# Quarter loads, an earlier third q, and k^T v portions moved between exchange and values in an attention and expert kernel

## The chip, the cores and the metric

One core of a Trainium2 chip. The metric is the device time of one run in microseconds; lower is better.

## What is computed

The reference has two parts, one feeding the other. The first is a linear attention over 8 batches, 8 heads, 576 tokens and 64 features per head, all in FP32:

```python
kv = np.einsum('bhsd,bhse->bhde', k, v)
out = np.einsum('bhsd,bhde->bhse', q, kv)
rms = np.sqrt(np.mean(out * out, axis=-1, keepdims=True) + 1e-06)
x = (out / rms * g_norm)            # then laid out as 4608 tokens of 512
```

The second is a mixture of 8 experts on those 4608 tokens. A token whose product with `w_skip` is not positive keeps its value. Every other token takes the expert with the largest logit, goes through `relu(x @ w1) @ w2` (512 to 1024 to 512), and adds the result weighed by its gate.

## The kernel before, in words

**Attention** takes the first 106 us or so. A token is 4 tiles wide: head pairs are two partition halves (`a`), and four pairs lie in the free dimension as `2u + w`. A load of one batch's k, v or q fills a tile of 128 partitions x 4 x 9 x 64 numbers (1.18 MB). `load_part` (L115 to L120) issues half of it, two of the four pairs, as one DMA of 576 KB on SyncE's queue (SP); `load_kv` issues the halves of k and v alternately, `load_q` the two of q. k and v have three buffers each, q has two. DMAs share eight completion semaphores in turn, so the issue of one waits on SP until the one eight places before it has landed.

Per batch b there are these pieces of work:

- `state(b, some)`, a **portion** of k^T v (L379): of the batch's 18 chunks it takes `some`, four matmuls of 64x64 for each (the trace shows eight passes, as FP32 takes two). The first nine chunks need the first half of k and v, the other nine the second. With the last chunk, ScalarE copies the sum out of PSUM (L386).
- `state_t(b)` transposes it (L393, then ScalarE's copy to kvT, L396), `state_m(b)` multiplies with the gate weights (L402, copy L405).
- `state_s(b)`, the **exchange** (L411, 64x64 tiles, then ScalarE's copies L415), puts each head pair's matrix on the other partition half as well. The batch's values need L415.

The values are taken in 36 units. Each batch has four (two groups of tokens, two head groups u); after four batches, two tail units take the ninth token group of all four. Units 0 to 15 are batches 0 to 3, 16 and 17 the tail, then 18 to 33 and 34, 35 in the same way. A batch's first units are thus 0, 4, 8, 12, 18, 22, 26, 30.

The order of work is written out by hand: TensorE (PE) runs what the program lists, in that order. One loop step n does:

```python
turn(n + 1)          # PE: transpose q (L460); ScalarE: copy qT (L463). None for tail units
root(n - 1)          # ScalarE: square root of the mean squares (L529)
jobs(n, "early")
values(n)            # PE: L479 and L498, or L508 for a tail unit; ScalarE: squares (L514)
jobs(n, "mid")
norm(n - 1)          # VectorE: reciprocal (L536), scale (L545), which frees the PSUM bank
squares(n)           # VectorE: sum of squares (L522)
jobs(n, "pe")
... jobs(n, "end")   # here also loads and stores are issued
```

`values(n)` writes one of two PSUM buffers (`o_ps`), freed by L545 of unit n - 2. `at(step, part, job)` puts a job into a step. `portions[b]` gives for batch b the step of its first portion and the number of chunks in each portion, one portion per step, all of them in part "pe", behind the values. The step after the last portion has `state_t` ("early") and `state_m` ("pe"); the next has the exchange, "early" when it is the batch's first unit, else "pe". `load_kv(b + 3)` goes to the end of the step with b's transpose (step 0 for batch 0), `load_q(b + 2)` to the end of the batch's third unit.

Beside this run, in VectorE's and GpSimd's time: the weighing of values by g_norm (L615), stores of x on SP (L650) and GpSimd (L646), and, from step 12 on, the choice of experts (`gating`: VectorE, and a ranking on PE, L693 to L699), a few instructions in each step. At the very start `dense` matmuls (L170) on constants fill PE's time between the first pieces of work.

**The experts** take the rest: tokens are gathered by indirect DMAs, the two layers run in `layer_1`, `layer_2`, `fast_1` and `fast_2` (L1176, L1188, L1256), and the weights of the next expert are loaded (L336, L346) when PE has done with their buffer.

Of the kernel before, what the change touches and what calls it, by code (L numbers as in the profile page):

```python
# [8 lines left out]
FP32 = mybir.dt.float32  # L9
# [8 lines left out]
def kernel(  # L18
# [44 lines left out]
    B, H, S, D = q.shape  # L63
    DM = H * D
    N = B * S
    P = 128
    C = S // 64
# [30 lines left out]
    kv_pool = attn.enter_context(tc.tile_pool(name="kv", bufs=3))  # L98
# [13 lines left out]

    kts, vts, qts = {}, {}, {}

    def load_part(t, src, b, u):  # L115

        js = slice(2 * u, 2 * u + 2)
        nc.sync.dma_start(
            out=t[:, js, :, :].rearrange("p j c d -> p j (c d)"),
            in_=src[b].rearrange("(j a) (p c) d -> (a p) j (c d)", a=2, c=C)[:, js, :])  # L120

    def load(pool, tag, src, b):
        t = pool.tile([P, 4, C, D], FP32, tag=tag, name=tag)
        for u in range(2):
            load_part(t, src, b, u)
        return t

    def load_kv(b):
        if b < B:
            for name, to in (("k", kts), ("v", vts)):  # L130
                to[b] = kv_pool.tile([P, 4, C, D], FP32, tag=name, name=name)
            for u in range(2):
                for src, t in ((k, kts[b]), (v, vts[b])):
                    load_part(t, src, b, u)

    def load_q(b):
        if b < B:
            qts[b] = load(q_pool, "q", q, b)
# [4 lines left out]


    load_kv(0)
    load_q(0)

# [19 lines left out]
    def dense(count, ps=warm_ps):  # L167

        for _ in range(count):
            nc.tensor.matmul(out=ps[:, :], lhsT=ones[:, :],  # L170
                             rhs=ones[:, :].unsqueeze(1).to_broadcast([P, 4, P]), start=True, stop=True)
# [33 lines left out]
    for i in range(KVD):  # L205
        t = kvd_pool.tile([P, 2, 2, 2, PK], FP32, name=f"kvd{i}")
# [87 lines left out]
    for lo, m, _ in runs:  # L294

        if m < P and (lo, m) not in again:
            t = keep.tile([P, P], FP32, name=f"again{lo}_{m}")
# [57 lines left out]
    def own(b, w):  # L355

        return kvds[b % KVD][w * 64:(w + 1) * 64, :, w, w, :]
# [7 lines left out]
    def ends_of(x):  # L365

        ap = [list(d) for d in x.ap]
        assert ap[-1] == [1, PK]
        return bass.AP(x.tensor, x.offset, ap[:-1] + [[PK - G, 2], [1, G]])

    def state(b, some):

        kt, vt = kts[b], vts[b]
        for i in some:
            u, c = divmod(i, C)
            for w in range(2):
                for a in range(2):
                    r = slice(a * 64, (a + 1) * 64)
                    nc.tensor.matmul(  # L379
                        out=sum_ps[w * 64:(w + 1) * 64, a, u, :],  # L380
                        lhsT=kt[r, 2 * u + w, c, :], rhs=vt[r, 2 * u + w, c, :],
                        start=(c == 0), stop=(c == C - 1), skip_group_check=True)
        if some.stop < 2 * C:
            return
        for w in range(2):
            nc.scalar.copy(out=own(b, w)[:, :, G:G + 2 * D].rearrange("p u (a d) -> p a u d", a=2),  # L386
                           in_=sum_ps[w * 64:(w + 1) * 64, :, :, :])

    def state_t(b):
        for u in range(2):  # L390
            for w in range(2):
                r = slice(w * 64, (w + 1) * 64)
                nc.tensor.matmul(out=kvT_ps[:, u, r], lhsT=kvds[b % KVD][:, u, w, w, G:G + 2 * D],  # L393
                                 rhs=ident[:, r], start=True, stop=True)
        kvT = att_pool.tile([P, 2, P], FP32, tag="kvT", name="kvT", bufs=1)
        nc.scalar.copy(out=kvT[:, :, :], in_=kvT_ps)  # L396
        kvTs[b] = kvT

    def state_m(b):
        kvT = kvTs.pop(b)  # L400
        for u in range(2):
            nc.tensor.matmul(out=lg_ps[:, u, :, :, :], lhsT=kvT[:, u, :], rhs=gw_b[:, u, :, :, :],  # L402
                             start=True, stop=True)
        for w in range(2):
            nc.scalar.copy(out=ends_of(own(b, w)), in_=lg_ps[w * 64:(w + 1) * 64, :, :, w, :])  # L405

    def state_s(b):

        for w in range(2):
            r, o = slice(w * 64, (w + 1) * 64), slice((1 - w) * 64, (2 - w) * 64)  # L410
            nc.tensor.matmul(out=sw_ps[o, :], lhsT=ident[r, r], rhs=own(b, w), start=True, stop=True,  # L411
                             skip_group_check=True)
        for w in range(2):
            o = slice((1 - w) * 64, (2 - w) * 64)
            nc.scalar.copy(out=kvds[b % KVD][o, :, w, 1 - w, :],  # L415
                           in_=sw_ps[o, :].rearrange("p (u k) -> p u k", u=2))
# [25 lines left out]
    def at(step, part, job):  # L442
        todo.setdefault((step, part), []).append(job)
# [7 lines left out]
    def turn(n):  # L451
        _, b, i, u = units[n]
        if i is None:
            qTs[n] = q8s[b][:, u, :, :, :]
            return
        ps = ps_q.tile([P, 2, 2, 2, 64], FP32, tag="q", name="q_ps")
        for w in range(2):
            for hf in range(2):
                c = 4 * i + 2 * hf
                nc.tensor.transpose(out=ps[:, w, :, hf, :], in_=qts[b][:, 2 * u + w, c:c + 2, :],  # L460
                                    identity=ident[:, :])
        qT = att_pool.tile([P, 2, 2, P], FP32, tag="qT", name="qT")
        nc.scalar.copy(out=qT[:, :, :, :].rearrange("p w a t -> p (w a t)"),  # L463
                       in_=ps[:, :, :, :, :].rearrange("p w a h t -> p (w a h t)"))
        qTs[n] = qT
# [353 lines left out]
    def slot_rows(cols, pool, tag):  # L819

        n = cols.stop - cols.start
        rows = pool.tile([P, n], I32, tag=f"rows{tag}", name="rows")
        nc.vector.tensor_single_scalar(out=rows[:, :], in_=srow[:, cols], scalar=float(N),
                                       op=ALU.add)
        src = pool.tile([P, n], I32, tag=f"src{tag}", name="src")
        nc.vector.scalar_tensor_tensor(out=src[:, :], in0=rows[:, :], scalar=N, in1=rows[:, :],
                                       op0=ALU.is_lt, op1=ALU.mult)
        return rows, src
# [64 lines left out]
    def early():  # L893
# [41 lines left out]
        yield "mid", put  # L935

    load_kv(1)
    load_q(1)
    load_kv(2)


# [7 lines left out]
    starts = {}  # L949
    for n, (_, b, i, _) in enumerate(units):  # L950
        if i is not None:
# [2 lines left out]
    dense(4)  # L954
    state(0, range(C, 2 * C))
    dense(5)
    turn(0)
    state_t(0)
    state_m(0)
    turn(1)  # L960
    state_s(0)

    portions = {1: (1, (10, 8)), 2: (4, (6, 6, 6)), 3: (7, (5, 6, 7)), 4: (11, (3, 4, 4, 4, 3)),
                5: (16, (3, 2, 6, 7)), 6: (20, (4, 4, 5, 5)), 7: (24, (4, 4, 5, 5))}
    over = 0
    for b, n in starts.items():
        if b:
            step, counts = portions[b]
            i = 0
            for count in counts:  # L970
                at(step, "pe", lambda b=b, some=range(i, i + count): state(b, some))
                i += count
                step += 1
            assert i == 2 * C and step < n and step - len(counts) > over - 1
            at(step, "early", lambda b=b: state_t(b))
            at(step, "pe", lambda b=b: state_m(b))
            at(step + 1, "early" if step + 1 == n else "pe", lambda b=b: state_s(b))
            over = step
        at(over, "end", lambda b=b: load_kv(b + 3))

        at(n + 2, "end", lambda b=b: load_q(b + 2))

    def gating(g):

        yield from choose(g)
        yield lambda: rank(g)
        numbers = number(g)
        yield next(numbers)
        if g == LAST - 1:
            yield from rank_experts()  # L990
            load_weights(0, wpool_a, later=True)
        yield from numbers
        if g == LAST - 1:
            yield from early()
# [60 lines left out]
    with tc.tile_pool(name="wpool_b", bufs=1, reuse_waits="tile") as wpool_b, \  # L1055
# [491 lines left out]
        rows, src = slot_rows(slice(0, NCOL), gat_pool, "")  # L1547
# [34 lines left out]
        with tc.If(n_rounds > 1):  # L1582
            with tc.For_i(1, n_rounds, 1):
# [12 lines left out]
                rows, src = slot_rows(slice(0, NCOL), slot_pool, "")  # L1596
# [35 lines left out]
```

## Time and profile before

| | |
|---|---|
| median of 3 runs | 374.82 us (374.59 to 375.59) |
| the profiled execution | 374.1 us, of which the span is 372.2 us |
| granted TensorE clock | 0.998 |
| TensorE matmul busy | 361.7 us, 97% of the span |
| VectorE, ScalarE, GpSimd busy | 243.4, 145.9, 119.9 us |
| loads of k, v, q | 16 DMAs each, 576 KB, median 10.0, 10.8, 10.7 us to landing |

Times in the profile count from the start of the span. A row of the timeline gives start, duration, engine, line, operation, tiles written and read, shape, the number of instructions merged, and in brackets the engine's idle time before it and the work that ended it.

### The profile page before, as it was taken

Reading aid. Unit: us, or ns where it says so; the run is one execution under the profiler, and the core shown is the slowest. Engines: PE = TensorE matmul, PEld = TensorE weight load, DVE = VectorE, ACT = ScalarE, POOL = GpSimd, SP = SyncE. Lnnn points to the kernel's source line nnn. Section 1 sums busy time; section 2 is a strip of 40 time slices with the busy share of each in tenths; the row PEclk is TensorE's granted clock in tenths of the full one; section 3 lists DMA queues with packets and bytes.
Section 4 is the critical chain, followed back from the end, with each engine's and each line's share of the span. In section 5 each row is a group of like instructions: output and inputs, shape, how many; then the busy total and the mean of one; then the engine's idle time right before and its main releaser. Section 6 shows DMA issues by size and latency. Waiting matters only on the chain.

```text
span 372.2 us, 9661 instructions
## 1 busy us (share of the span) xinstructions
PE 361.7 (97%) x3859; PEld 314.4 (84%) x3859; DVE 243.4 (65%) x630; ACT 145.9 (39%) x398; POOL 119.9 (32%) x189
## 2 busy tenths in 40 slices
PE   8999999999999999999999999999999999999994
PEld 4687797898979779689879987998988998999983
DVE  3355367767788753875856685876876876878831
ACT  2466576676777132224303511431430440441420
POOL 7035467655767253223022303303202302102003
PEclk9999999999999999999999999999999999999999
DMA  8999999997489449974608264672762762601001
GB/s 289 393 391 390 402 404 395 406 393 232 135 316 311 115 119 324 397 249 168 224 32 274 64 227 139 205 242 75 253 233 48 276 232 55 257 3 42 16 1 54
DMA packets 32039, 81.70 MB, mean 219 GB/s; under 512 B 2474, under 2 KB 2482, under 8 KB 31988
## 3 DMA queue, kind: packets, MB, share of 16 engines
q1 hardware_dynamic: 28176, 69.47, 52.5%
q0 software_dynamic: 3792, 11.53, 9.2%
q8 instruction: 32, 0.52, 0.6%
q14 instruction: 19, 0.16, 0.1%
q10 hardware_dynamic: 20, 0.02, 0.0%
HBM read 66.80 MB, written 14.48 MB: 218 GB/s over the span
## 4 chain that ended last, share of the span: by engine, by line
PE 87%; issue 5%; ACT 3%; POOL 2%; DVE 1%; POOLq 0%; ACTq 0%; DVEq 0%
PE bank L1256 45%; PE bank L1188 9%; PE o_ps L498 7%; PE sum_ps L379 5%; PE q_ps L460 4%; PE bank L1176 4%; PE g_ps L393 2%; PE q_ps L170 2%; PE bank L1157 2%; PE g_ps L856 1%; PE g_ps L411 1%; ACT qT L463 1%; PE o_ps L508 1%; PE q_ps L856 1%; PE g_ps L402 1%
## 5 line engine op out<-in xcount | busy, mean ns | idle before, releaser
L1266 ACT COPY p<-bank 128x128 f32<-128x128 f32 (+6 forms) x70 | 20.8, 297 | 99.4 <-PE bank L1256 97.6
L1256 PE MATMUL bank<-xt,w 128*128 128x128 f32 (+5 forms) x336 | 55.4, 288 | 0.0
L1387 POOL DMA_INDIRECT out_dram<-xg,rows x14 | 14.0, 999 | 119.5 <-DVE xg L1384 108.4
L615 POOL TENSOR_TENSOR xb<-xl,g_b 128x512 f32<-128x512 f32 x34 | 41.3, 1216 | 32.1 <-DVE rs L536 30.3
L1256 PEld LDWEIGHTS bank<-xt,w 128*128 128x128 f32 x336 | 47.0, 190 | 1.9 <-DVE bank L1260 1.4
L1260 DVE TENSOR_TENSOR bank<-bank,p 128x128 f32<-128x128 f32 (+6 forms) x70 | 23.5, 336 | 30.3 <-PE bank L1256 29.4
L498 PE MATMUL o_ps<-kvd,qT 128*128 128x146 f32 x240 | 35.8, 290 | 1.0 <-ACT kvd L415 0.7
L1256 PE MATMUL bank<-xs,s 128*128 128x128 f32 (+5 forms) x224 | 36.7, 288 | 0.0
L522 DVE TENSOR_REDUCE rs<-sq 128x8 f32<-128x512 f32 x36 | 24.6, 682 | 14.5 <-ACT sq L514 14.4
L498 PEld LDWEIGHTS o_ps<-kvd,qT 128*128 128x128 f32 x240 | 31.5, 188 | 2.0 <-ACT kvd L415 1.5
L1256 PEld LDWEIGHTS bank<-xs,s 128*128 128x128 f32 x224 | 31.1, 190 | 1.0 <-ACT p L1266 0.8
L1188 PE MATMUL bank<-w,ht 128*32 128x128 f32 (+2 forms) x424 | 29.9, 313 | 0.0
L545 DVE TENSOR_TENSOR xl<-o_ps,rs 128x584 f32<-128x584 f32 x32 | 24.5, 767 | 4.3 <-DVE rs L536 0.5
L1188 PEld LDWEIGHTS bank<-w,ht 128*32 128x32 f32 (+2 forms) x424 | 18.2, 119 | 10.7 <-issue 7.6
L1256 PE MATMUL bank<-t,ht 128*128 128x256 f32 x112 | 27.0, 384 | 0.0
L1256 PE MATMUL bank<-w,ht 128*128 128x256 f32 x112 | 26.5, 380 | 0.0
L514 ACT ACTIVATE sq<-o_ps 128x512 f32<-128x512 f32 x34 | 20.3, 597 | 15.0 <-PE o_ps L498 14.4
L1148 POOL DMA_INDIRECT xg<-out_dram,src x14 | 15.3, 1092 | 33.0 <-DMA out_dram<-xg,rows 17.3
L1256 PE MATMUL bank<-t,hs 128*128 128x256 f32 x112 | 25.3, 379 | 0.0
L379 PE MATMUL sum_ps<-v,k 64*64 64x64 f32 x1152 | 24.7, 223 | 0.4 <-issue 0.4
L379 PEld LDWEIGHTS sum_ps<-v,k 64*64 64x64 f32 x1152 | 20.9, 134 | 4.3 <-issue 1.8
L1256 PEld LDWEIGHTS bank<-t,ht 128*128 128x128 f32 x112 | 20.8, 190 | 3.9 <-issue 1.2
(224 smaller groups left out, 677.2 us busy)
## 6 DMA issues: line engine op xcount, KB each, us to landing
w<-in_moe_w_dram SPq DMA_DIRECT2D x16, 2048.0 KB, 8.9
k<-in_k_dram SPq DMA_DIRECT2D x16, 576.0 KB, 10.0
v<-in_v_dram SPq DMA_DIRECT2D x16, 576.0 KB, 10.8
q<-in_q_dram SPq DMA_DIRECT2D x16, 576.0 KB, 10.7
out_dram<-xb SPq DMA_DIRECT2D x29, 256.0 KB, 9.4
out_dram<-xb POOLq DMA_DIRECT2D x7, 256.0 KB, 6.4
xg<-out_dram,src POOLq DMA_INDIRECT x16, 3.7
out_dram<-xg,rows POOLq DMA_INDIRECT x16, 5.9
```

The costliest lines, as they stand in the source:

```text
L379: nc.tensor.matmul(out=sum_ps[w * 64:(w + 1) * 64, a, u, :], lhsT=kt[r, 2 * u + w, c, :], rhs=vt[r, 2 * u + w, c, :], start=(c == 0), stop ...
L460: nc.tensor.transpose(out=ps[:, w, :, hf, :], in_=qts[b][:, 2 * u + w, c:c + 2, :], identity=ident[:, :])
L498: mm = nc.tensor.matmul(out=ps[:, w, 0:2 * PK].rearrange("p (r k) -> p r k", r=2)[:, :, cols], lhsT=qT[:, w, a, :], rhs=kvds[b % KVD][:, u ...
L514: nc.scalar.activation(out=sq[:, :, :, :], in_=heads(ps, G, G + 2 * D), func=ACT.Square)
L522: nc.vector.tensor_reduce(out=rs[:, :, :], in_=sq[:, :, :, :].rearrange("p x y (a d) -> p x (y a) d", a=2), axis=AX.X, op=ALU.add)
L545: nc.vector.tensor_tensor(out=xl[:, :, :, :].rearrange("p x y (a k) -> p x (y a) k", a=2), in0=ps[:, :, 0:2 * PK].rearrange("p x (h k) -> ...
L615: late.append((lambda eng: eng.tensor_tensor(out=xb[:, :, 4 * u * D:(4 * u + 4) * D].rearrange("p r (w x) -> p r w x", w=2), in0=xl[:, :, ...
L1148: nc.gpsimd.indirect_dma_start(out=x_of(xg, off, m), out_offset=None, in_=cut_rows(m)[:, :], in_offset=bass.IndirectOffsetOnAxis(ap=idx[:, ...
L1188: nc.tensor.matmul(out=yps[q * m:(q + 1) * m, 0:n], lhsT=ht(f)[:, off:off + m], rhs=w_sb[r][1][:, f, q * n:(q + 1) * n], start=(f == 0), s ...
L1256: nc.tensor.matmul(out=out, lhsT=lhsT(i), rhs=rhs(i), start=start and i == 0, stop=i == k - 1, skip_group_check=True)
L1260: nc.vector.tensor_tensor(out=to, in0=x, in1=y, op=ALU.add)
L1266: nc.scalar.copy(out=t, in_=x)
```

## The change

Loads: each of k, v and q comes in quarters of 288 KB, one pair each, instead of halves. Batch 3's k and v are issued in two parts: the first two quarters of each where all of it was, the other two behind the third q (batch 2's).

Order: at the start `state_t(0)` stands ahead of `turn(0)`. The first portions of batch 2 (step 4), batch 3 (step 8) and batch 5 (step 16) move from behind the step's values to ahead of them; in steps 4 and 8 that is behind the exchange. Batch 4 has three portions (5, 6, 7 chunks) instead of five, so that its transpose, multiplication and exchange come two steps earlier (14 and 15), and so does the issue of batch 7's k and v. Batch 5's portions hold 8, 4, 3, 3 chunks instead of 3, 2, 6, 7. The last batch's transpose goes behind the values of its step, and its multiplication into the next step, behind that step's turn.

```diff
-    def load_part(t, src, b, u):
-        js = slice(2 * u, 2 * u + 2)
+    def load_part(t, src, b, j):
+        js = slice(j, j + 1)
...
-        for u in range(2):
-            load_part(t, src, b, u)
+        for j in range(4):
+            load_part(t, src, b, j)
...
-    def load_kv(b):
+    def load_kv(b, js=range(4)):
         if b < B:
-            for name, to in (("k", kts), ("v", vts)):
-                to[b] = kv_pool.tile([P, 4, C, D], FP32, tag=name, name=name)
-            for u in range(2):
+            if js.start == 0:
+                for name, to in (("k", kts), ("v", vts)):
+                    to[b] = kv_pool.tile([P, 4, C, D], FP32, tag=name, name=name)
+            for j in js:
                 for src, t in ((k, kts[b]), (v, vts[b])):
-                    load_part(t, src, b, u)
+                    load_part(t, src, b, j)
...
+    state_t(0)
     turn(0)
-    state_t(0)
     state_m(0)
...
-    portions = {1: (1, (10, 8)), 2: (4, (6, 6, 6)), 3: (7, (5, 6, 7)), 4: (11, (3, 4, 4, 4, 3)),
-                5: (16, (3, 2, 6, 7)), 6: (20, (4, 4, 5, 5)), 7: (24, (4, 4, 5, 5))}
+    portions = {1: (1, (10, 8)), 2: (4, (6, 6, 6)), 3: (7, (5, 6, 7)), 4: (11, (5, 6, 7)),
+                5: (16, (8, 4, 3, 3)), 6: (20, (4, 4, 5, 5)), 7: (24, (4, 4, 5, 5))}
...
-                at(step, "pe", lambda b=b, some=range(i, i + count): state(b, some))
+                at(step, "early" if step in (starts[1], starts[2], starts[4] - 2) else "pe",
+                   lambda b=b, some=range(i, i + count): state(b, some))
...
-            at(step, "early", lambda b=b: state_t(b))
-            at(step, "pe", lambda b=b: state_m(b))
+            last = b == B - 1
+            at(step, "mid" if last else "early", lambda b=b: state_t(b))
+            at(*((step + 1, "early") if last else (step, "pe")), lambda b=b: state_m(b))
...
-        at(over, "end", lambda b=b: load_kv(b + 3))
+        at(over, "end", lambda b=b: load_kv(b + 3, range(4 if b else 2)))
         at(n + 2, "end", lambda b=b: load_q(b + 2))
+        if b == 0:
+            at(n + 2, "end", lambda: load_kv(3, range(2, 4)))
```

## The prediction

> **What bounds the kernel now.** I read the page's busy shares first, then the chain that ended last, then TensorE's timeline of the attention stage, and last its waits and the DMA landings.
>
> ```profile
> PE 361.7 (97%) x3859; PEld 314.4 (84%) x3859; DVE 243.4 (65%) x630; ACT 145.9 (39%) x398; POOL 119.9 (32%) x189
> DMA  8999999997489449974608264672762762601001
> PE 87%; issue 5%; ACT 3%; POOL 2%; DVE 1%; POOLq 0%; ACTq 0%; DVEq 0%
> ```
>
> TensorE (PE) is busy 97% of the 372.2 us and holds 87% of the chain, so a microsecond taken from its row of work in attention (0 to about 106 us) should come off the end. But the DMA row is full in the same place: 392 GB/s or so for the first 84 us, one 2304-byte packet taking 94 ns on each of 16 engines. So I must ask whether the loads let PE run earlier.
>
> Busy PE hides small losses, so I compare start times. Batch 2's first values, timeline of PE:
>
> ```profile
> 28.12 0.71 PE L411 MATMUL g_ps<-kvd,ident 64*64 64x292 f32 x4 [0.19 <-ACT kvd L405]
> 28.76 0.44 PE L479 MATMUL o_ps<-ident,q 128*128 128x128 f32 x2
> 29.38 1.27 PE L498 MATMUL o_ps<-kvd,qT 128*128 128x146 f32 x8 [0.18 <-ACT kvd L415]
> 30.58 0.93 PE L379 MATMUL sum_ps<-v,k 64*64 64x64 f32 x48
> 31.44 0.66 PE L460 MATMUL q_ps<-ident,q 128*128 128x128 f32 x4
> ```
>
> From the exchange (L411) to the next turn (L460) are 3.32 us: L411 0.64, L479 with the wait for ScalarE's copies 0.62, values 1.20, the k^T v portion 0.86. Where a portion already follows an exchange, it reads:
>
> ```profile
> 79.74 0.46 PE L411 MATMUL g_ps<-kvd,ident 64*64 64x292 f32 x2
> 79.75 0.44 PE L379 MATMUL sum_ps<-v,k 64*64 64x64 f32 x6
> 80.04 0.41 PE L411 MATMUL g_ps<-kvd,ident 64*64 64x292 f32 x2
> 80.28 0.63 PE L379 MATMUL sum_ps<-v,k 64*64 64x64 f32 x26
> 80.84 0.65 PE L460 MATMUL q_ps<-ident,q 128*128 128x128 f32 x4
> ```
>
> Both work on 64x64 tiles and interleave: 1.10 us for an exchange and 32 passes, and each further pass costs about 15 ns (48 passes alone take 0.86, 32 take 0.63). A portion between 128-row work pays about 0.09 us before its first pass, 0.08 in it and 0.14 after it (intervals of 216, 87 and 149 ns where 125 and 7 are usual).
>
> Around the tail of the first four batches, and at the start:
>
> ```profile
> 60.71 1.24 PE L498 MATMUL o_ps<-kvd,qT 128*128 128x146 f32 x8 [0.24 <-DVE xl L545]
> 63.04 1.19 PE L393 MATMUL g_ps<-ident,kvd 128*128 128x64 f32 x8 [0.58 <-ACT kvd L386]
> ...
> 12.36 0.66 PE L460 MATMUL q_ps<-ident,q 128*128 128x128 f32 x4
> 12.86 1.00 PE L393 MATMUL g_ps<-ident,kvd 128*128 128x64 f32 x8
> 14.32 0.64 PE L402 MATMUL g_ps<-gw_b,kvT 128*128 128x36 f32 x4 [0.46 <-ACT kvT L396]
> ```
>
> **What the Trainium skill says.** "TensorEngine Tiling (Array Packing)", Tiling Modes, Key Properties: changing the tiling mode drains TensorE. The trace agrees: that is the 0.31 us per isolated portion. "Perfetto Trace Analysis", opening note: matmul busy time is a bad measure, because matmuls are pipelined. It agrees here: the last L479 starts 0.46 before L498, where 0.11 is usual, and of the 0.35 lost the timeline shows 0.18 as idle. "DMA: Bandwidth & Descriptors", Anatomy of one DMA: about 2 us per DMA are fixed and the semaphore write is nearly free. The trace has 3.99 us for the first k half, of which 1.5 are its packets, so 2.5 fixed; the 4-byte semaphore packet takes 9 ns.
>
> **The change part by part.**
>
> *Start.* turn(0) (four L460, 0.5 us) goes behind state_t(0). PE reaches L393 at 12.36 instead of 12.86; the copies it needs (L386) ended at 11.95. ScalarE's kvT copy, now ahead of the qT copy, and L402 come 0.5 earlier, and turn(0) fills the wait that was idle. Gain 0.5.
>
> *Step 4 (batch 2) and step 8 (batch 3).* The portion goes between exchange and values. Exchange and 48 passes: 1.10 + 16 x 0.015 = 1.34; L479 0.22; values 1.00 as they now meet a turn: 2.56. The wait is covered: ScalarE's first copy ended 1.2 after L411's start, and values now come 1.56 after it. Step 4 gives 3.32 - 2.56 = 0.76. Step 8 took 3.42 (41.07 to 44.49): 0.86.
>
> *Steps 11 to 19.* Batch 4 takes 5, 6, 7 chunks in three steps instead of five portions; its state_t moves from step 16 to 14, where turn(15) covers the wait for L386; batch 5 puts 8 chunks ahead of values(16). From 52.12 (exchange of step 11) to step 20's turn at 74.33 are 22.21 us. Rebuilt from pieces: step 11 1.23, step 12 2.66, step 13 2.78, step 14 3.09 (as 24.23 to 27.29), step 15 values 1.10 and exchange with 64 passes 1.58, step 16 0.67 + ranking 0.71, step 17 1.92, steps 18 and 19 2.32 each: 20.38, so 1.83 less. It consists of two portions' switches (0.62), the 0.8 at L393 (by start times; 0.58 is shown) less its new 0.16, the 0.45 for a PSUM bank that VectorE frees late (L545), and interleaving. What is late next is VectorE: following L522, L529 and L545 through these steps, bank releases come within 0.1 us of values(15), (16) and (17), the ranking waits some 0.15 for its one-hot, and values(18) some 0.2. I take 0.4 off (bounds 0 and 0.9): 1.4.
>
> ScalarE's copies move along with it (L396, L405, L415, four at most in a step) and are in these sums.
>
> *Last batch.* state_t(7) behind values(28) avoids 0.23 us for L386, but L402 then waits for kvT behind a square: 0.1.
>
> *Loads.* 48 half loads become 96 quarters (288 KB), same packets. SP pays about 0.4 us per issue against 0.75 us of data: it keeps up. 48 x 16 semaphore packets of 9 ns over 16 engines are 0.4 us by 84 us. Each issue waits for the one eight before it, so queued data falls from some 12 to 6 us; with 2.5 us fixed that still feeds the engines. What lies behind a waiting load on SP are later loads and the stores; xb has six buffers, and POOL shows no wait for one. At the start, four quarters fly first; the gate load's landing (3.30) releases the fifth, whose data can start at about 5.2, before the first four end at about 5.6. So no bubble, but v0's second half, which starts PE's second row at 9.84 (landed 9.71), may slip: 0 to 0.5 (a gain is excluded, since as many bytes stand ahead of it), I take 0.2. The third q goes ahead of k3 and v3's second half: its first half landed at 36.39 and turn(8) started at 36.55. A PE running 1.1 us earlier would have waited for it; now it lands 3 us sooner. The halves put back landed at 33.4 and 34.9 and come 3 us later, about 38; step 8 needs them near 40. So this edit is worth nothing alone and protects the rest. The next tight ones are v1's second half (19.68, needed now near 20.2) and q3 (47.11, needed near 48.4); later loads have over 4 us. Batch 7's loads are issued at the end of step 14 instead of 16 and pass one store on SP: nothing, for v7 landed at 79.66 and is needed after 85, and the store's buffer is not asked for.
>
> *Sum.* 0.5 + 0.76 + 0.86 + 1.4 + 0.1 - 0.2 = 3.4 us. Against the profiled execution (372.2 us span, 1.9 around it, 374.1) that is 370.7; the median is 374.82, 0.7 above it, so I forecast 371.4. The expert stage, with weights fetched by waits on PE, should just move.
>
> **Rivals.** (1) *VectorE becomes the bound in steps 12 to 19, or early loads hold PE.* If the rebuilt region gives only 0.5 instead of 1.4, and v1 or q3 hold PE for 0.8: 3.4 - 0.9 - 0.8 = 1.7, so 373.1. For it: the bank releases above are close. Against: VectorE is busy 16.5 of 22.2 us there. (2) *Slower: smaller loads starve the DMA engines.* If 288 KB at a time lowers the rate, q3 lands late in proportion: (47.11 - 2.6) x loss, against 1.3 of slack and 3.6 of gain. It decides from 11% (below some 350 GB/s); at 15% q3 is 6.7 late and the time is 374.8 - 3.6 + 5.4 = 376.6. For it: SP can be held by a PE or POOL wait with only half the cover. Against: SP's waits in this stretch are on landings, and 6 us exceed 2.5. (3) *Nothing arrives:* another wait at the end of attention, such as the gather for the first expert (landed 111.21, used 112.49), takes the gain: 374.8. Against: it is itself issued from PE's work.
>
> **How the numbers follow.** Forecast 0.62, rival 1 0.26, rival 2 0.06, rival 3 0.06. The forecast's own span is 370.6 to 372.4 (gain 2.4 to 4.2). The range reaches to rival 1 with its spread: 370.5 to 373.3. About 0.3% (1.1 us) is what a measurement can tell from no change. Faster takes the forecast and nearly all of rival 1: 0.87; within 0.3% 0.07; slower 0.06.
>
> **What would show it.** Right: L402 near 13.8; no L415 wait at batches 2 and 3; L393 of batch 4 near 57 without 0.58 idle; step 20's turn near 71; the same packets at 390 GB/s. Wrong: idle ahead of L379 or L460 on a landing, VectorE waits at L498 and L479 in steps 15 to 19, or an attention stage 3 us shorter with the end unmoved.

## The result, and the profile after

| | before | changed |
|---|---|---|
| median of 22 runs each | 374.79 us (373.79 to 375.77) | 372.94 us (370.67 to 374.87) |
| the profiled execution | 374.1 us, span 372.2 | 371.14 us, span 369.3 |
| TensorE matmul busy | 361.7 us | 359.9 us |

The ratio is 0.9946, with a 95% interval of 0.9933 to 0.996. The changed kernel is 1.85 us faster by the medians. The two profiled executions lie 2.96 us apart: that of the changed kernel fell 1.8 us below its own median, that of the kernel before 0.7. Most of the forecast's working came true, piece by piece, and yet its sum of 3.4 us did not arrive.

The page's rows for TensorE, DMA and the chain hardly differ from those of before:

```profile
PE 359.9 (97%) x3859; PEld 314.8 (85%) x3859; DVE 242.8 (66%) x630; ACT 146.2 (40%) x398; POOL 118.9 (32%) x189
DMA  8999999999588449973617355564662772601001
PE 86%; issue 5%; DMA 2%; ACT 2%; DVE 2%; POOL 1%; SPq 0%; POOLq 0%; DVEq 0%; ACTq 0%
```

PE keeps its 97% and the DMA row stays full; the new 2% of DMA in the chain is a first sign that data comes late. The rest is seen in start times. Step 4, timeline of PE (start, duration, then the work):

```profile
27.43 0.46 PE L412 MATMUL g_ps<-kvd,ident 64*64 64x292 f32 x2 [0.19 <-ACT kvd L406]
27.55 0.41 PE L380 MATMUL sum_ps<-v,k 64*64 64x64 f32 x4
27.73 0.41 PE L412 MATMUL g_ps<-kvd,ident 64*64 64x292 f32 x2
27.78 1.06 PE L380 MATMUL sum_ps<-v,k 64*64 64x64 f32 x44
28.77 0.44 PE L480 MATMUL o_ps<-ident,q 128*128 128x128 f32 x2
29.05 1.17 PE L499 MATMUL o_ps<-kvd,qT 128*128 128x146 f32 x8
30.05 0.60 PE L461 MATMUL q_ps<-ident,q 128*128 128x128 f32 x4
```

From the exchange to the next turn are 2.62 us where 3.32 were: the 48 passes run in the exchange's shadow, and the values no longer wait for ScalarE. Now the start, and steps 14 to 20:

```profile
9.61 0.33 PE L380 MATMUL sum_ps<-v,k 64*64 64x64 f32 x4
10.15 1.26 PE L380 MATMUL sum_ps<-v,k 64*64 64x64 f32 x68 [0.22 <-DMA v<-in_v_dram]
...
12.44 1.00 PE L394 MATMUL g_ps<-ident,kvd 128*128 128x64 f32 x8
...
13.90 0.64 PE L403 MATMUL g_ps<-gw_b,kvT 128*128 128x36 f32 x4
...
57.19 1.19 PE L394 MATMUL g_ps<-ident,kvd 128*128 128x64 f32 x8
...
66.44 0.41 PE L480 MATMUL o_ps<-ident,q 128*64 128x128 f32 x2 [0.24 <-DVE xl L546]
66.68 0.54 PE L499 MATMUL o_ps<-kvd,qT 128*128 128x146 f32 x3
67.93 0.89 PE L499 MATMUL o_ps<-kvd,qT 128*128 128x146 f32 x5 [0.71 <-issue]
...
72.41 1.28 PE L394 MATMUL g_ps<-ident,kvd 128*128 128x64 f32 x8 [0.17 <-ACT kvd L387]
```

L403 has lost the 0.46 of idle time that L402 had, and the transpose of batch 4 (57.19) its 0.58. Three things are new. The second row of k^T v breaks off after four passes: v0's last quarter landed at 10.02, its half had landed at 9.71. The transpose at 72.41 waits for ScalarE's copy. And in the middle of one unit's values PE stands still for 0.7 us with nothing that the profile can name ("issue"): no semaphore, no data.

### The profile page after: what moved, and what is told of

Its sections match the earlier page's. It is cut to its first block, busy times and chain, and to the rows that moved or that the text cites. A ratio compares the mean times of both kernels' runs of the same rounds, so it can differ in the third digit from the quotient of the medians.

```text
span 369.3 us, 9717 instructions
## 1 busy us (share of the span) xinstructions
PE 359.9 (97%) x3859; PEld 314.8 (85%) x3859; DVE 242.8 (66%) x630; ACT 146.2 (40%) x398; POOL 118.9 (32%) x189
## 4 chain that ended last, share of the span: by engine, by line
PE 86%; issue 5%; DMA 2%; ACT 2%; DVE 2%; POOL 1%; SPq 0%; POOLq 0%; DVEq 0%; ACTq 0%
PE bank L1261 45%; PE bank L1193 9%; PE o_ps L499 8%; PE sum_ps L380 5%; PE bank L1181 4%; PE q_ps L461 4%; DMA v<-in_v_dram 2%; PE g_ps L394 2%; PE bank L1162 2%; PE g_ps L412 1%; PE o_ps L480 1%; PE g_ps L857 1%; ACT sq L515 1%; PE g_ps L403 1%; PE q_ps L857 1%
## 5 line engine op out<-in xcount | busy, mean ns | idle before, releaser
L1271 ACT COPY p<-bank 128x128 f32<-128x128 f32 (+6 forms) x70 | 20.8, 297 | 99.0 <-PE bank L1261 97.5
L499 PE MATMUL o_ps<-kvd,qT 128*128 128x146 f32 x240 | 36.0, 290 | 0.9 <-issue 0.7
L499 PEld LDWEIGHTS o_ps<-kvd,qT 128*128 128x128 f32 x240 | 31.6, 189 | 1.6 <-issue 0.9
L1153 POOL DMA_INDIRECT xg<-out_dram,src x14 | 14.1, 1006 | 35.4 <-DMA out_dram<-xg,rows 18.6
L380 PE MATMUL sum_ps<-v,k 64*64 64x64 f32 x1152 | 25.3, 222 | 0.2 <-DMA v<-in_v_dram 0.2
L380 PEld LDWEIGHTS sum_ps<-v,k 64*64 64x64 f32 x1152 | 21.6, 134 | 3.6 <-issue 0.9
L1261 PEld LDWEIGHTS bank<-t,ht 128*128 128x128 f32 x112 | 20.8, 190 | 3.9 <-issue 1.2
```

The costliest lines, as they stand in the source:

```text
L380: nc.tensor.matmul(out=sum_ps[w * 64:(w + 1) * 64, a, u, :], lhsT=kt[r, 2 * u + w, c, :], rhs=vt[r, 2 * u + w, c, :], start=(c == 0), stop ...
L499: mm = nc.tensor.matmul(out=ps[:, w, 0:2 * PK].rearrange("p (r k) -> p r k", r=2)[:, :, cols], lhsT=qT[:, w, a, :], rhs=kvds[b % KVD][:, u ...
L1261: nc.tensor.matmul(out=out, lhsT=lhsT(i), rhs=rhs(i), start=start and i == 0, stop=i == k - 1, skip_group_check=True)
L1271: nc.scalar.copy(out=t, in_=x)
```

## The experiments

Ratios are to the kernel before, run beside it on the same chip; its median was 375.02 us in the e runs, 376.55 in the f runs and 376.61 in the g runs, so ratios are to be compared across these groups, not times. "Stretch 11 to 20" is the time from the start of values(11) to that of values(20): 24.99 us before, 24.83 in the changed kernel.

### What the loads and the moved portions do

**e1_halves**: the changed order with half loads, the third q between the two halves of batch 3's k and v.

```diff
-        js = slice(j, j + 1)
+        js = slice(2 * u, 2 * u + 2)
...
-        at(over, "end", lambda b=b: load_kv(b + 3, range(4 if b else 2)))
+        at(over, "end", lambda b=b: load_kv(b + 3, range(2 if b else 1)))
...
-            at(n + 2, "end", lambda: load_kv(3, range(2, 4)))
+            at(n + 2, "end", lambda: load_kv(3, range(1, 2)))
```

> The changed order of work with loads in halves of 576 KB, as before; the third q still goes between the two halves of batch 3's k and v. Changed kernel: 372.9 us, before: 374.8. Theory A (the quarters cost time: in the changed kernel's trace v0's last quarter lands at 10.02 instead of 9.71 and v1's last at 20.43 instead of 19.68): the order alone gives about 371.6, ratio to before 0.9915, with v0 landed near 9.7 and v1 near 19.7. Theory B (the loads are neutral; VectorE's bank releases and stalls in TensorE's own issue take the missing 1.5 us): 372.9, ratio 0.995.

Measured: 373.15 us, ratio 0.9955 (0.994 to 0.997). That halves would regain time was wrong. In its profile v0's second half landed at 10.08, no earlier than v0's last quarter in the changed kernel's (10.02).

**e2_loads_only**: the kernel before with the changed kernel's loads and nothing of its order.

```diff
...
-        at(over, "end", lambda b=b: load_kv(b + 3))
+        at(over, "end", lambda b=b: load_kv(b + 3, range(4 if b else 2)))
...
+        if b == 0:
+            at(n + 2, "end", lambda: load_kv(3, range(2, 4)))
```

> The loads alone: quarters and the earlier third q, the order of TensorE's work as before. Theory A: slower than before, by 0.4 to 1.3 us (375.2 to 376.1), the start late on v0 and batch 1's first portion late on v1. Theory B: 374.8, within 0.3.

Measured: 374.73 us, ratio 0.9998 (0.9983 to 1.0012). By themselves the new loads neither cost nor gain anything that shows.

**e3_batches_4_5_back**: the changed kernel with batches 4 and 5 portioned as before.

```diff
-    ... 4: (11, (5, 6, 7)), 5: (16, (8, 4, 3, 3)), ...
+    ... 4: (11, (3, 4, 4, 4, 3)), 5: (16, (3, 2, 6, 7)), ...
...
-                at(step, "early" if step in (starts[1], starts[2], starts[4] - 2) else "pe",
+                at(step, "early" if step in (starts[1], starts[2]) else "pe",
```

> The changed kernel with batch 4's five portions and batch 5's 3, 2, 6, 7 chunks behind the values again. The prediction priced this part at 1.4 us: 374.3. Theory B (VectorE and issue stalls hold steps 12 to 19, where the changed kernel's trace came out only 0.4 us ahead): worth 0.5 or less, 373.0 to 373.4.

Measured: 372.3 us, ratio 0.9945 (0.9916 to 0.9974), no slower than the changed kernel; its stretch 11 to 20 took 24.98 us. Had the part brought 1.4 us, the ratio without it would be 0.998, outside this interval: it brings less, in the two profiles 0.15 us, and by the intervals a gain of some 1 us isn't excluded. Its profile has none of the "issue" stalls.

**e4_q2_late**: the changed kernel with the third q behind all of batch 3's k and v.

```diff
-        at(over, "end", lambda b=b: load_kv(b + 3, range(4 if b else 2)))
+        at(over, "end", lambda b=b: load_kv(b + 3))
...
-        if b == 0:
-            at(n + 2, "end", lambda: load_kv(3, range(2, 4)))
```

> The changed kernel with the third q behind all of batch 3's k and v again, still in quarters. The prediction said that the earlier q protects the rest: turn(8) wants it at 35.3 in the changed trace, where it landed at 33.9; three us later it holds TensorE for 1.0 to 1.6 us, so 374.0 to 374.5. Rival: the edit does nothing, 372.9.

Measured: 373.81 us, ratio 0.9968 (0.9957 to 0.998). Timeline of PE in e4_q2_late:

```profile
37.03 0.41 PE L461 MATMUL q_ps<-ident,q 128*128 128x128 f32 x2 [1.03 <-DMA q<-in_q_dram]
37.69 0.44 PE L461 MATMUL q_ps<-ident,q 128*128 128x128 f32 x2 [0.25 <-DMA q<-in_q_dram]
```

turn(8) waits for q twice. The edit protects some 0.8 us (ratio 0.9946 against 0.9968; the intervals barely overlap), a little less than the 1.0 to 1.6 expected.

### What the "issue" stalls are

The page's list of queues shows a small one that no line of the kernel issues; here of the changed kernel (packets, MB, share of 16 engines):

```profile
q8 instruction: 32, 0.52, 0.5%
```

Each packet is 16 KB, and they come about 126 matmul records apart. The Trainium skill ("Runtime: NRT & Kernel Launch", Instruction fetch mechanics) says that each engine fetches its instructions in 16 KiB blocks of 256 through a DMA queue of its own, and that crossing from one block to the next is mostly hidden. The size agrees: 126 matmuls with their weight loads are 252 instructions. So does the count: 32 packets for 3859 matmuls (30.6 times 126), 44 for 5499 in g1_shifted_few_loads (43.6 times). Most borders between blocks cost nothing that shows here, but some do. Up to 110 us the fourteen profiles have fifteen pauses of 0.45 us or more that no wait explains, in eleven of the kernels. In all fifteen PE went on 1.20 to 1.56 us after one of these packets had ended, and each lay within five of a matmul number 219 + 126n (counted from 0, the last one before the pause): 345 in the kernel before (0.56 us), 1227 in the changed one (0.87) and in e1_halves, e4_q2_late and f1_batch5_spread (0.55, 0.46, 0.53). I call these places borders. In the changed kernel the border ahead of 1227 is passed at 62.18, the packet moves from 65.55 to 66.63, PE stops at 66.9 and goes on at 67.93. This reads as a race between PE, which uses up a block, and the packet with the next one; g1_shifted_few_loads below tests it. The stretch around the stall in windows, before and then after:

```profile
62.00:67.00 5.00, 4.36 (x110) 3.89 (x111) 3.23 (x7) 2.82 (x8) 3.32 (x7) 1.00 1.04 404
```

```profile
62.00:67.00 5.00, 4.71 (x152) 4.06 (x144) 4.56 (x14) 3.52 (x8) 3.95 (x7) 1.00 1.05 405
```

After the window and its length come PE's busy time and count: 152 matmuls in these 5 us where there were 110. The last two columns, DMA share and GB/s, say that the DMA engines were full in both.

**f1_batch5_spread**: fewer passes in a row at step 16.

```diff
-    ... 5: (16, (8, 4, 3, 3)), ...
+    ... 5: (16, (5, 5, 4, 4)), ...
```

> The changed kernel, with batch 5's four portions of 5, 5, 4, 4 chunks instead of 8, 4, 3, 3; the first still stands ahead of values(16). Theory C (instruction fetch): 64 passes of 7 ns in a row ahead of a tail unit use up TensorE's instructions faster than its own DMA queue brings them, which is the issue stall of 0.87, 0.55 and 0.46 us near the 1227th matmul of the attention stage in three kernels with that order. With 40 passes there instead of 64 the stall goes or falls below 0.2, steps 11 to 19 take some 24.0 us instead of 24.3 to 24.8, and the time is 372.4. Theory V (VectorE): the stretch is bound by the PSUM banks that VectorE frees (0.61 us of waits in the changed kernel's profile); shorter work ahead of values(16) makes the wait for a bank longer by about 0.35 (24 passes), and the time stays at 372.9 to 373.2.

Measured: 373.56 us, ratio 0.993 (0.9903 to 0.9958); stretch 24.60 us. Timeline of PE:

```profile
69.05 0.57 PE L380 MATMUL sum_ps<-v,k 64*64 64x64 f32 x21 [0.32 <-issue]
```

The stall did not fall below 0.2 as expected: it is still there (0.53), at matmul 1227, but now within another piece of work. So the length of one portion isn't its cause.

**f2_shifted**: the same work with 63 more matmuls in front (and 9 more just before the experts).

```diff
         for _ in range(count):
-            nc.tensor.matmul(out=ps[:, :], lhsT=ones[:, :],
-                             rhs=ones[:, :].unsqueeze(1).to_broadcast([P, 4, P]), start=True, stop=True)
+            for x in range(4):
+                nc.tensor.matmul(out=ps[:, x * P:(x + 1) * P], lhsT=ones[:, :],
+                                 rhs=ones[:, :], start=True, stop=True)
```

> The changed kernel with each warming matmul of 512 columns split into four of 128: the same columns, some 63 more matmuls in TensorE's program before the attention's first values, so that every border between two blocks of TensorE's instructions moves by that many. All data work is as it was. Theory C: the issue stalls move with the borders: none at the 1227th matmul of the changed kernel's count, if any then some 63 earlier in the work (near the ranking or in step 15), and the time is within 0.6 us of 372.9 either way. Rival: the stall belongs to the place (the first values after the 64 passes), so it is there again at the same matmul of step 17, 0.4 to 0.9 us.

Measured: 378.3 us (375.03 to 383.42), ratio 1.0038 (1.0021 to 1.0055; it leaves out the three longest of the 22, 380.66 us and up). Timeline of PE:

```profile
12.20 0.23 PE L172 MATMUL q_ps<-ones 128*128 128x128 bf16 x1
14.48 1.22 PE L172 MATMUL q_ps<-ones 128*128 128x128 bf16 x19 [2.05 <-issue]
...
35.66 0.44 PE L462 MATMUL q_ps<-ident,q 128*128 128x128 f32 x2
36.73 0.44 PE L462 MATMUL q_ps<-ident,q 128*128 128x128 f32 x2 [0.63 <-issue]
...
68.05 0.47 PE L510 MATMUL o_ps<-kvd,q 64*64 64x73 f32 x11
70.40 0.54 PE L510 MATMUL o_ps<-kvd,q 64*64 64x73 f32 x19 [1.89 <-issue]
```

The stalls stand at matmuls 219, 596 and 1228 of this program's own count, so with the borders, and in other work than before (L510 of unit 17 instead of L499 of unit 18). Their sum against the usual intervals is 5.1 us (2.19, 0.80, 2.10). That the time would stay near 372.9 was wrong: a few small matmuls more, and the changed kernel loses all that it had gained. The stalls are the largest single part of it, but less than half: this span, 1.65 us above the kernel's median, is 8.9 us longer than the changed kernel's, of which 4.2 are stalls (5.1 less 0.87) and 2.9 lie behind the attention stage; and the clock was granted in full from 9.8 us only and by half from 71.2 to 74.6.

**g1_shifted_few_loads**: f2_shifted without the loads of later batches.

```diff
     def load_kv(b, js=range(4)):
-        if b < B:
+        if 3 <= b < B:
+            kts[b], vts[b] = kts[b - 3], vts[b - 3]
+        elif b < B:
...
     def load_q(b):
-        if b < B:
+        if 2 <= b < B:
+            qts[b] = qts[b - 2]
+        elif b < B:
```

> f2_shifted (split warming matmuls) without the loads of k and v of batches 3 to 7 and of q of batches 2 to 7: these batches use again the tiles of three (k, v) and two (q) batches before, so their data is another and the loads' traffic ends near 25 us. Theory C2 (a block of TensorE's instructions is asked for one block ahead, and waits behind the load data that already stands in the DMA engines): with the traffic gone after about 25 us, the issue stalls of f2_shifted near matmul 597 (0.80 us) and 1228 (2.10 us) fall below 0.2, the blocks come within 1.5 us of their request instead of 2.3 to 3.7, and the one near matmul 219, which lies at 12 us with the loads still flying, stays at 1 to 2.2. Rival (the stall belongs to the border itself, traffic or not): 597 and 1228 stall as in f2_shifted.

Timeline of PE:

```profile
11.31 0.23 PE L176 MATMUL q_ps<-ones 128*128 128x128 bf16 x1
12.78 1.22 PE L176 MATMUL q_ps<-ones 128*128 128x128 bf16 x19 [1.24 <-issue]
...
34.04 0.66 PE L466 MATMUL q_ps<-ident,q 128*128 128x128 f32 x4
...
65.77 0.74 PE L514 MATMUL o_ps<-kvd,q 64*64 64x73 f32 x32
```

Where loads still fly (12 us) the stall stays; the other two are gone, at the same borders in the same work. Near 1228 the packet moved 0.6 us after the border ahead of it, in f2_shifted 3.7 us. So the late packets come from the traffic of the loads, and not from the border or the work at it. (The whole run took 712 us, as the experts had other tokens.)

**g2_few_loads** and **g3_before_few_loads**: the same edit in the changed kernel and in the kernel before.

> The changed kernel without the loads of k and v of batches 3 to 7 and of q of batches 2 to 7, as in g1; the experts then work on other tokens, so only the attention stage is compared. From the start of values(11) to that of values(20), against g3 (the kernel before with the same left out): if late instructions took what the prediction's term for steps 11 to 19 lacks, the stretch is 1.1 to 1.4 us shorter here than in g3 (some 23.7 against 24.9). If VectorE's banks and ScalarE's copies took it, it is 0.3 to 0.7 shorter, as it was with the loads.

> The kernel before without the same loads. Values(11) to values(20) take 24.9 us, as with the loads (its profile had no late block in that stretch); the late block at 23 us (0.56) goes or shrinks; values(1) to values(20) take some 57.2 instead of 57.5.

| without later loads | values(3) to (5) | values(7) to (9) | stretch 11 to 20 |
|---|---|---|---|
| g3, order of before | 6.27 us | 6.97 | 24.98 |
| g2, changed order | 5.52 | 6.08 | 23.84 |
| gain | 0.75 | 0.89 | 1.14 |

With the loads away the moves of batches 4 and 5 earn 1.14 us, and with them 0.16 in the two profiles of before and after; of the 0.98 between, 0.87 is the stall at matmul 1227. The late block at 23 us did not go in either (0.53 in g3, 1.02 in g2): the first batches' loads were still flying then.

### Which part of the new order exposes what

**f3_batch_5_back**: batch 4 as changed, batch 5 as before.

```diff
-    ... 5: (16, (8, 4, 3, 3)), ...
+    ... 5: (16, (3, 2, 6, 7)), ...
...
-                at(step, "early" if step in (starts[1], starts[2], starts[4] - 2) else "pe",
+                at(step, "early" if step in (starts[1], starts[2]) else "pe",
```

> The changed kernel with batch 5's portions as before (3, 2, 6, 7 chunks, behind the values); batch 4 keeps its three portions and the earlier transpose. The prediction's pieces: two switches 0.62 and 0.64 at the transpose stay, the 0.45 for the bank and its 0.4 price go, so steps 11 to 19 gain 1.2 on before (23.8 instead of 25.0 us) and the time is 371.7 to 372.0. Theory C agrees, and adds that no issue stall is to be seen near the 1227th matmul. Theory V: the bank waits of steps 15 to 18 eat the gain of batch 4 as well, the stretch takes 24.5 or more, and the time is 372.6 to 373.0.

Measured: 373.91 us, ratio 0.9937 (0.9917 to 0.9957); stretch 24.64 us, not 23.8. Timeline of PE:

```profile
64.01 0.74 PE L509 MATMUL o_ps<-kvd,q 64*64 64x73 f32 x32 [0.82 <-DVE xl L546]
...
68.36 0.41 PE L480 MATMUL o_ps<-ident,q 128*64 128x128 f32 x2 [0.50 <-DVE xl L546]
```

VectorE frees the banks late and takes batch 4's gain. Against the usual intervals values(16) lose 1.22 us here and unit 18's L480 0.66. In the changed kernel, where batch 5's eight chunks lie ahead of them, values(16) lose nothing that shows, values(17) 0.21 and unit 18's L480 0.41. The two moves belong together. By its ratio this kernel is nevertheless not behind the changed one; differences of half a microsecond are not told apart by these intervals.

**f4_halves_old_4_5**: e3_batches_4_5_back with the half loads of e1_halves (the loads' lines as in e1_halves).

> The changed kernel with half loads (the third q still between the halves of batch 3's k and v) and with the portions of batches 4 and 5 as before: only the start's order, steps 4 and 8 and the last batch's order are left of the moves. By the pieces seen so far (0.65, 0.76, 0.86, 0.1 to 0.3, and no late quarter at the start) it gains 2.4 to 2.6: 372.4 to 372.6. If the late last quarter of v0 (0.43 to 0.6 us in the quarters' profiles) costs what it shows, it is 0.4 to 0.6 below the same kernel with quarters (372.3 in its seven runs), so 371.8; if it doesn't, 372.3 to 372.5.

Measured: 374.98 us, ratio 0.9962 (0.9951 to 0.9974), so 1.4 us gained where 2.4 or more was expected. Its profile shows why, at the same place as in e1_halves, whose timeline of PE reads:

```profile
43.60 0.49 PE L461 MATMUL q_ps<-ident,q 128*128 128x128 f32 x3
45.13 0.27 PE L461 MATMUL q_ps<-ident,q 128*128 128x128 f32 x1 [1.04 <-issue]
```

At border 723 both half kernels lose 1.21 us: their packet moves 5.5 us after the border ahead of it (37.1 and then 42.6 in e1_halves). With quarters it moves after 3.3 to 4.0 us in the five kernels with the new order of steps 4 and 8, the early q and the same borders (the changed one, e3, f1, f3, g4), and they lose at most 0.14 there. Over the borders 345 to 1227 the mean is 4.0 and 3.8 us in the two half kernels, 2.5 to 2.7 in the changed kernel and e3; but e4_q2_late, with quarters too, has 3.4. In the profiles, then, quarters win about a microsecond at that border by letting instructions through sooner. What they lose by late data is less sure. Batch 1's first portion takes 1.39 or 1.40 us in all four profiles with halves and 1.41 to 1.95 in the ten with quarters. But v0 is not late with quarters alone: f4_halves_old_4_5, too, waits for it (timeline of PE), although none was expected:

```profile
10.19 1.28 PE L380 MATMUL sum_ps<-v,k 64*64 64x64 f32 x72 [0.66 <-DMA v<-in_v_dram]
```

The times of e1_halves and the changed kernel differ by less than the intervals.

**g4_transposes_behind**: f1_batch5_spread, with the last batch's placing of transpose and multiplication given to batches 5 and 6 too.

```diff
-            last = b == B - 1
+            last = b >= 5
```

> The changed kernel with batch 5's portions of 5, 5, 4, 4 chunks (f1_batch5_spread) and with the transposes of batches 5 and 6 behind their step's values and the multiplication behind the next turn, as the last batch has it. At steps 20 and 24 the transpose waits 0.22 to 0.34 and 0.37 us for ScalarE's copy in the profiles so far; these waits go, and the multiplication waits up to 0.1 for its copy in turn. Expected 0.4 us below f1_batch5_spread: a ratio of 0.992 to the kernel before. If the copy of the product then comes late for the exchange, or late instructions grow by as much, it stays at 0.993 to 0.995.

Measured: 373.72 us, ratio 0.9929 (0.9902 to 0.9956). Timeline of PE at steps 20 and 24:

```profile
73.10 1.17 PE L499 MATMUL o_ps<-kvd,qT 128*128 128x146 f32 x8
...
84.75 1.27 PE L499 MATMUL o_ps<-kvd,qT 128*128 128x146 f32 x8 [0.20 <-DVE xl L546]
```

Values(20) follow the turn at once and the wait for ScalarE is gone; at step 24 a wait for VectorE's bank takes its place. The 0.4 us that this was to gain on f1_batch5_spread (0.993) do not show. f1_batch5_spread and this one have the lowest ratios of all, but neither is shown to beat the changed kernel (0.9946, 0.9933 to 0.996): the intervals overlap.

## Why the prediction was right and wrong

The direction and the range held. That the range held is in part luck: 372.94 lies outside the forecast's own span (370.6 to 372.4), in the part that had been added for rival 1 (373.1), and little of what brought it there is shown to be what rival 1 named. By the prediction's own steps:

- **Start, 0.5.** From the last pass of the second row of k^T v to values(0), 5.85 us became 5.21 in the changed kernel, e1, e3 and e4, and stayed 5.85 in e2_loads_only: 0.64.
- **Step 4, 0.76, and step 8, 0.86.** 0.75 and 0.89 in g2 against g3; with the loads 0.76, and 1.08 at step 8, of which 0.19 is a pause at border 723 of the kernel before.
- **Steps 11 to 19, 1.4.** Between the two points that the prediction used (exchange of step 11, step 20's turn) g3 takes 22.22 us and g2 20.81; the forecast was 20.38 + 0.4 = 20.8. The sum is right to the hundredth, but not in every piece, so the last hundredths are luck: VectorE's waits came to 0.62, not 0.4. With the loads the changed kernel takes 21.79 us, of which 0.87 is the stall. And the sum ended one instruction too early. Step 20's transpose, just behind the turn, now waits for ScalarE's copy (it starts 0.45 us after the turn's last matmul in the changed kernel, 0.17 before), since step 19 got shorter; 1.14 is left. "What is late next is VectorE" missed that.
- **Last batch, 0.1.** The gain grows from 2.49 us at values(20) to 2.78 at values(31): 0.1 by values(30), as forecast, and 0.2 more because L921, 0.2 us late at 105.8 us in the kernel before, no longer is (L922 of the changed kernel).
- **Loads, -0.2: the step that failed.** It asked how late the data would be, and put 0 to 0.5 on v0. In this profile v0's last quarter cost 0.43 and v1's 0.24 (its portion takes 1.64 us instead of 1.40), 0.67 where 0.2 stood; for v0 it isn't shown that the quarters are the cause, as halves came as late in e1_halves and f4_halves_old_4_5. (The 2 us per DMA that it cites stand in a section on GpSimd's path; these loads go through SP's queue, and for them the 2.5 us that it measured count.) And it didn't ask who else uses the DMA engines: "6 us exceed 2.5" and "early loads hold PE" speak of data alone. TensorE's own instructions come through the same engines, late while the loads run, and the change makes PE use them up faster: 0.87 us at one stall, for which the sum had no term.

For the two profiled executions the account nearly closes: 0.64 + 0.75 + 0.89 + 1.14 + 0.3 - 0.67 is 3.05, and the stalls of 0.87 in place of 0.56 leave 2.74; values(31) come 2.78 us earlier, and the spans differ by 2.96. For the medians it closes only in kind. They differ by 1.85, and what the other runs lost has no profile. Late instructions may do it: f2_shifted spreads over 5.4 us even without its three longest runs (though its longer runs also tend to a lower granted clock), and the changed kernel over 4.2, where the kernel before spread over 2.0 beside it and 2.5 in the f runs. A clock that is granted late, as in the last section, may do it too: it costs some 0.6 to 1.0 us, and the two profiles of this account are free of it. How much of the missing microsecond belongs to either is open.

Rival 1's first half, VectorE as the bound, is what f3_batch_5_back shows without batch 5's new portions; of its second, v1 or q3 holding PE for 0.8 us, the 0.24 at v1 came; rival 2 did not happen (379 to 399 GB/s in slices 2 to 9 of the page, 390 to 406 before; PE waits for no landing after the two late quarters). The signs named in advance came: L403 at 13.90, no wait of values for the copies in steps 4 and 8, the transpose at 57.19, the turn at 71.58; and of the signs against, idle time ahead of L380 on a landing and a VectorE wait at L480.

## What to carry to other kernels

Where TensorE is dense and the DMA engines are full, as here, its instructions are a transfer too, and can come late: count how many it uses between two packets of the instruction queue, and look for "issue" idle time in the middle of a uniform group, some 1.2 to 1.6 us behind such a packet. Removing waits ahead of such a place can turn them into an instruction stall; loads in smaller pieces let the packets through sooner in most of the profiles here, and adding or removing instructions anywhere earlier moves the places. When a stretch is rebuilt from pieces, carry the sum one instruction past the stretch's end, to the first wait whose cover has become shorter.

## What was not expected of the hardware

- TensorE's instruction packets (16 KB) moved 2.5 to 4.0 us, on average of a kernel, after the border ahead of them while loads ran at some 390 GB/s, and mostly under 1 us, 2.2 at most, once the loads were gone (g1, g2, g3, 33 to 95 us). A late one cost up to 2.19 us.
- The full TensorE clock is granted at different times from one execution to the next: from 5.0 us on in the changed kernel's profile, from 10.3 in e1_halves, 9.8 in e3 and 10.1 in g4. In these three the first 72 passes of k^T v took 1.8 to 1.9 us instead of 1.06, and values(0) started at 17.2 to 17.4 instead of 16.4; PE then came too late to wait for v0. It shows with the order of before too (g3, 10.4), so it does not need the change; whether the change makes it more frequent can't be told from fourteen profiles.
